# A small row copy moved into free bytes of the last weight slot, and the order of the final matmuls pinned (one Trainium2 core, one-token decode block)

## The chip, the cores and the metric

The kernel runs on one core of one Trainium2 chip. The metric is the device time of one execution in microseconds (us). In the profile PE is the TensorE matmul engine, PEld its weight loads, DVE is VectorE, ACT is ScalarE, SP issues most transfers. "Half clock" means that the clock granted to TensorE was 0.5 of full speed; the trace records each such period.

Each execution has two lengths: the time (outside view) and the span (first to last instruction in the records). All runs quoted were classed fast.

## The reference

One new token `x` (1 x 1024) goes through two branches that are added:

```python
xn = layernorm(x)
# A: grouped-query attention; 32 query heads, 4 key/value heads, 65536 cached keys, Dh = 128
q = xn @ wq;  p = softmax(q @ k.T * Dh**-0.5);  a = (p @ v) @ wo
# B: a mixer, then an MLP with w3 (1024 x 3584) and w4 (3584 x 1024)
h  = gelu(layernorm(xn) @ w1);  x1 = xn + (h, shifted) @ w2
b  = x1 + gelu(layernorm(x1) @ w3) @ w4
out = x + a + b
```

Nearly all of it is reading caches and weights: 169.87 MB for a single row of output.

## The kernel before

Weights and caches come through three slots of 64 KB per partition, one after another in one DMA queue. The last items are the last key block, `wo`, the last value block V7, and `w4` in eight pieces. The slot of `w4` is the one the last key block leaves.

```python
W4_PIECES = (6, 5, 6, 4, 3, 2, 1, 1)      # rows of w4 per transfer, 28 in all
# ...
    def row_acc(j, lhsT, rhs, start=False):
        nc.tensor.matmul(psB[32 * j:32 * j + 32, :], lhsT=lhsT.to_broadcast([lhsT.shape[0], 32]), rhs=rhs, start=start,
                         stop=False, tile_position=(0, 32 * j), skip_group_check=True)
# ... the final value block, inside compute_v
        for e in range(SUBS):
            for t in range(16):
                q = t % 4
                nc.tensor.matmul(oacc[32 * q:32 * (q + 1), :], lhsT=pT[:, e, 32 * t:32 * (t + 1)],
                                 rhs=vt[:, :, e, t, :], start=(e == 0 and t < 4),
                                 stop=(e == SUBS - 1 and t >= 12), tile_position=(0, 32 * q))
        st.done(("V", u))
# ...
        nc.vector.scalar_tensor_tensor(out=og[:], in0=oacc[:], scalar=wb[:, 1:2], in1=og[:],
                                       op0=ALU.mult, op1=ALU.add)
        group_rows(g, og, ol)
```

`row_acc` adds rows into the output accumulator `psB`. `group_rows` masks and sums `og` on DVE (`ol`), gathers the sums over partitions with one matmul (`pm_e`), and normalises to `oT` for the last head group. Before that, `o_acc` collects the output projection of the other three head groups; `add_projection` copies it out of PSUM and adds it to `psB`.

```python
    def add_projection():
        rows = ppool.tile([1, 2, 512], F32, name="o_rows", tag="p")
        nc.vector.tensor_copy(out=rows[:], in_=tail["rows"][0:1, 0:2, :])
        for j in range(2):
            row_acc(j, ident_f[0:1, 0:1], rows[0:1, j, :])

    def compute_w4(lo, hi):
        wt = st.tiles["w4"]
        for c in range(lo, hi):
            for j in range(2):
                row_acc(j, hT[:, c:c + 1], wt[:, D * c + 512 * j:D * c + 512 * (j + 1)])
# ...
    compute_k(NU - 1)
    tail["rows"] = ps_S.tile([P, SUBS, 512], F32, name="o_acc", tag="sc")
    for g in range(HKV - 1):
        project(g)
    add_projection()
    compute_v(NU - 1)
    early = sum(W4_PIECES[:2])
    compute_w4(0, early)
    project(HKV - 1)
    compute_w4(early, FC - NARROW)
```

The tile `o_rows` comes from pool `psb`, tag `p`. It has a single buffer, and this buffer holds `p_sb`, the softmax weights that the value matmuls read. So the copy must wait for the last value matmul. After `psB` a short tail follows: `psB` is copied to `sums`, added to the last six `w4` rows in `pm_r`, cast, stored.

Of the kernel before, what the change touches and what calls it, by code (L numbers as in the profile page):

```python
# [9 lines left out]
F32 = mybir.dt.float32  # L10
# [7 lines left out]
SUBS = 4  # L18
SETS = 4
SLOTS = 3  # L20
W4_PIECES = (6, 5, 6, 4, 3, 2, 1, 1)
NARROW = 6
AHEAD = 3

# [70 lines left out]
def kernel(  # L95
# [14 lines left out]
    nc = tc.nc  # L110
# [3 lines left out]
    D = A_x.shape[-1]  # L114
    S = A_x.shape[1]
    HKV = A_k_cache.shape[1]
    SK = A_k_cache.shape[2]
    DH = A_k_cache.shape[3]
# [3 lines left out]
    FC = F // P  # L122
    UKEYS = P * ROW // DH
    assert DH == P and HQ // HKV == 8 and HKV == 4 and D == 1024 and F == 3584 and S == 1
    assert SK % UKEYS == 0 and sum(W4_PIECES) == FC
    NB = SK // UKEYS
    NU = HKV * NB
# [6 lines left out]
    ppool = ctx.enter_context(tc.tile_pool(name="psb", bufs=1))  # L134
# [14 lines left out]
    class Stream:  # L149
# [17 lines left out]
        def load(self, it):  # L167
# [13 lines left out]
            elif it == "w4":  # L181
                w4_v = B_w4.rearrange("(m c) n -> m c n", c=FC)
                c0 = 0
                for n in W4_PIECES:
                    go(out=t[:, c0 * D:(c0 + n) * D], in_=w4_v[:, c0:c0 + n, :].rearrange("p c n -> p (c n)"))
# [7 lines left out]
    st = Stream()  # L193
# [6 lines left out]
    ident_f = const.tile([P, P], F32, name="ident_f")  # L200
# [9 lines left out]
    for b in range(2):  # L210
        nc.gpsimd.tensor_copy(
            out=spread[:, 2 * b:2 * b + 2, :].rearrange("p r (a i) -> p r a i", a=4),
            in_=ident_f[:, 64 * b:64 * b + 64].rearrange("p (i r) -> p r i", r=2).unsqueeze(2).to_broadcast([P, 2, 4, 32]))
# [6 lines left out]
    psB = ps_B.tile([P, 512], F32, name="psB")  # L220

    def row_acc(j, lhsT, rhs, start=False):
        nc.tensor.matmul(psB[32 * j:32 * j + 32, :], lhsT=lhsT.to_broadcast([lhsT.shape[0], 32]), rhs=rhs, start=start,  # L223
                         stop=False, tile_position=(0, 32 * j), skip_group_check=True)

    x_t = ppool.tile([P, DC, 32], BF16, name="x_t", tag="p")
    for a in range(4):
        nc.vector.transpose(out=x_t[32 * a:32 * a + 32].rearrange("p c j -> p (c j)"),  # L228
                            in_=x_row[:, 256 * a:256 * (a + 1)].rearrange("p (i c) -> p c i", c=DC))
# [3 lines left out]
    def layernorm(src, tag):  # L233
# [37 lines left out]
    sel8big = const.tile([P, P], F32, name="sel8big")  # L271
    nc.vector.tensor_copy(out=sel8big[:].rearrange("p (h d) -> p h d", d=16),
                          in_=sel8[:].unsqueeze(2).to_broadcast([P, 8, 16]))
# [8 lines left out]
    for j in range(2):  # L282
        row_acc(j, ident_f[0:1, 0:1], accx[0:1, 512 * j:512 * (j + 1)], start=True)
# [104 lines left out]
    def group_weights():  # L388
        nball = group["nball"]
        negmg = small.tile([P, 1], F32, name="negmg")  # L390
        nc.vector.tensor_reduce(out=negmg[:], in_=nball[:], axis=AX.X, op=ALU.min)
        wb = small.tile([P, NB], F32, name="wb")
        nc.scalar.activation(out=wb[:], in_=nball[:], func=ACTF.Exp, bias=negmg[:, 0:1], scale=-1.0)
        og = group["og"]
        nc.vector.tensor_scalar(out=og[:], in0=og[:], scalar1=wb[:, 0:1], scalar2=None, op0=ALU.mult)
        lw = small.tile([P, NB], F32, name="lw")
        ol = small.tile([P, DH + 1], F32, name="ol")
        nc.vector.tensor_tensor_reduce(out=lw[:], in0=group["lall"][:], in1=wb[:], scale=1.0, scalar=0.0,
                                       op0=ALU.mult, op1=ALU.add, accum_out=ol[:, DH:DH + 1])
        return og, wb, ol  # L400
# [3 lines left out]
    def compute_v(u):  # L404
        g, b = divmod(u, NB)
        if b == 1:
            og, wb, ol = group_weights()
        vt = st.tiles[("V", u)][:].rearrange("p (s u t d) -> p s u t d", u=SUBS, s=SETS, t=16)
        oacc = ps_O.tile([P, 512], F32, name="oacc")
        pT = group["p"]  # L410
        for e in range(SUBS):
            for t in range(16):
                q = t % 4
                nc.tensor.matmul(oacc[32 * q:32 * (q + 1), :], lhsT=pT[:, e, 32 * t:32 * (t + 1)],  # L414
                                 rhs=vt[:, :, e, t, :], start=(e == 0 and t < 4),
                                 stop=(e == SUBS - 1 and t >= 12), tile_position=(0, 32 * q))
        st.done(("V", u))
        if b == 0:
            og = ogpool.tile([P, 512], F32, name="og", tag="og")
            nc.scalar.copy(out=og[:], in_=oacc[:])  # L420
            group["og"] = og
            return
        nc.vector.scalar_tensor_tensor(out=og[:], in0=oacc[:], scalar=wb[:, 1:2], in1=og[:],  # L423
                                       op0=ALU.mult, op1=ALU.add)
        group_rows(g, og, ol)

    oT = {}
    tail = {}

    def group_rows(g, og, ol):  # L430
        pe = ps_M.tile([P, 512], F32, name="pm_e", tag="pm")
        own = og[:].rearrange("p (s d) -> p s d", d=DH)
        nc.vector.tensor_tensor(out=own, in0=own, in1=mask4[:].unsqueeze(2).to_broadcast([P, 4, DH]), op=ALU.mult)
        nc.vector.tensor_reduce(out=ol[:, 0:DH], in_=og[:].rearrange("p (s d) -> p d s", d=DH), axis=AX.X, op=ALU.add)  # L434
        nc.tensor.matmul(pe[:, 0:DH + 1], lhsT=sel8big[:], rhs=ol[:], start=True, stop=True)  # L435
        msk = small.tile([P, 16, 8], F32, name="msk", tag="msk")
        nc.vector.tensor_tensor(out=msk[:], in0=pe[:, 0:P].rearrange("p (dd j) -> p dd j", j=8),
                                in1=mask16[:].unsqueeze(2).to_broadcast([P, 16, 8]), op=ALU.mult)
        o5 = small.tile([P, 8], F32, name="o5")
        nc.vector.tensor_reduce(out=o5[:], in_=msk[:].rearrange("p dd j -> p j dd"), axis=AX.X, op=ALU.add)  # L440
        rl = small.tile([P, 1], F32, name="rl")
        nc.vector.reciprocal(out=rl[:], in_=pe[:, P:P + 1])
        oT[g] = const.tile([P, 8], BF16, name=f"oT{g}")
        nc.vector.tensor_scalar(out=oT[g][:], in0=o5[:], scalar1=rl[:, 0:1], scalar2=None, op0=ALU.mult)

    def project(g):
        wt = st.tiles["wo"][:].rearrange("p (g j n) -> p g j n", g=HKV, j=8)
        for j in range(8):
            for h2 in range(2):
                if g == HKV - 1:  # L450
                    row_acc(h2, oT[g][:, j:j + 1], wt[:, g, j, 512 * h2:512 * (h2 + 1)])
                    continue
                nc.tensor.matmul(tail["rows"][0:1, h2, :], lhsT=oT[g][:, j:j + 1],  # L453
                                 rhs=wt[:, g, j, 512 * h2:512 * (h2 + 1)], start=(g == 0 and j == 0),
                                 stop=(g == HKV - 2 and j == 7), tile_position=(0, 0))

    def add_projection():
        rows = ppool.tile([1, 2, 512], F32, name="o_rows", tag="p")
        nc.vector.tensor_copy(out=rows[:], in_=tail["rows"][0:1, 0:2, :])  # L459
        for j in range(2):  # L460
            row_acc(j, ident_f[0:1, 0:1], rows[0:1, j, :])

    def compute_w4(lo, hi):
        wt = st.tiles["w4"]
# [3 lines that stand above are left out]
# [4 lines left out]
    for u in range(NU - 1):  # L472
        compute_k(u)
        compute_v(u)
    compute_k(NU - 1)
    tail["rows"] = ps_S.tile([P, SUBS, 512], F32, name="o_acc", tag="sc")
    for g in range(HKV - 1):
        project(g)
    add_projection()
    compute_v(NU - 1)  # L480
    early = sum(W4_PIECES[:2])
    compute_w4(0, early)
    project(HKV - 1)
    compute_w4(early, FC - NARROW)
    sums = ogpool.tile([64, 512], F32, name="sums", tag="og")
    nc.scalar.copy(out=sums[:], in_=psB[0:64, :])
    quarters = [ps_M.tile([P, 512], F32, name="pm_r", tag="pm") for _ in range(2)]
# [1 line left out]
    def quarter_acc(lhsT, rhs, start=False):  # L489
        for h in range(2):  # L490
            for j in range(2):
                q = 2 * h + j
                nc.tensor.matmul(quarters[h][32 * q:32 * q + 32, 0:256], lhsT=lhsT(j), rhs=rhs(j, h), start=start, stop=False,
                                 tile_position=(0, 32 * q), skip_group_check=True)

    def narrow_rows(lo, hi, start=False):
        wt = st.tiles["w4"]
        for c in range(lo, hi):
            quarter_acc(lambda j: hT[:, c:c + 1].to_broadcast([P, 32]),
                        lambda j, h: wt[:, D * c + 512 * j + 256 * h:D * c + 512 * j + 256 * (h + 1)],  # L500
                        start=start and c == lo)

    narrow_rows(FC - NARROW, FC - NARROW + AHEAD, start=True)
    quarter_acc(lambda j: ident_f[0:64, 32 * j:32 * j + 1].to_broadcast([64, 32]),
                lambda j, h: sums[:, 256 * h:256 * (h + 1)])
    narrow_rows(FC - NARROW + AHEAD, FC)

# [4 lines left out]
                        in_=out_t[31:33].rearrange("p h n -> p (h n)"))  # L512
# [29 lines left out]
```

## Time and profile before

| | before |
|---|---|
| time, median of the first three runs | 401.93 us (400.98 to 401.99) |
| span of the profiled execution | 399.0 us |
| mean DMA rate over the span | 426 GB/s |
| PE / DVE / ACT busy | 59% / 52% / 7% |

From the page of the kernel before: the span, the busy share of the DMA engines in 40 slices (tenths, 9 means 90% or more), and the chain of work that ended last, by line.

```profile
span 399.0 us, 2590 instructions
...
DMA  9998999999999999999999999999999999999996
...
DMA big<-in_A_k_cache_dram 42%; DVE big L359 19%; PE sc L364 8%; DMA big<-in_A_wq_dram 5%; PE oacc L414 5%; PE o_acc L453 3%; DVE mx L369 3%; ACT p_sb L382 3%; DVE p_sb L385 2%; PE psB L223 2%; PE psq L289 1%; DVE m L373 0%; PE pm_mx L371 0%; PE pm_mx L378 0%
...
```

DMA is busy at 9 in 38 of 40 slices, so the stream sets the pace of the whole. The chain line does not contradict this: it follows releasers, and inside the stream it goes through waits on slots.

The tail, from the timeline of the kernel before. Columns: start us, length us, engine, line, operation, output<-input, count; the bracket gives the idle time before and who ended it.

```profile
...
384.41 1.21 DVE L459 COPY o_rows<-o_acc 1x1024 f32<-1x1024 f32 x1 [14.25 <-PE oacc L414]
385.55 0.73 DVE L423 SCALAR_TENSOR_TENSOR og<-oacc,wb,og 128x512 f32<-128x512 f32 x1
...
385.68 1.05 PE L223 MATMUL psB<-o_rows,ident_f 1*32 1x512 f32 x4 [1.33 <-DVE o_rows L459]
...
386.65 1.95 PE L223 MATMUL psB<-big,hT 128*32 128x512 bf16 x10
...
388.53 0.80 PE L435 MATMUL pm_e<-ol,sel8big 128*128 128x129 f32 x2
...
395.46 0.58 ACT L486 COPY sums<-psB 64x512 f32<-64x512 f32 x1 [27.91 <-PE psB L223]
...
396.66 0.51 PE L493 MATMUL pm_r<-big,hT 128*32 128x256 bf16 x12
...
397.25 0.43 DVE L510 CAST out_t<-pm_r 64x256 bf16<-64x256 f32 x1 [6.91 <-PE pm_r L493]
...
```

The copy (L459) starts 0.02 us after the last value matmul, which ends at 384.39. PE then idles 1.33 us for it, and `og` (L423), which needs only the value matmuls, stands behind it on DVE and starts 1.14 us late. The chain of waits of the same kernel over the tail (start us, length us, what):

```profile
...
384.41 1.22 DVE o_rows L459
...
385.68 2.92 PE psB L223 x14
388.60 0.73 PE pm_e L435 x2
389.33 5.57 PE psB L223 x45
...
395.46 0.59 ACT sums L486
...
396.09 1.13 PE pm_r L493 x20
...
397.25 0.43 DVE out_t L510
```

No DMA appears in it. The landing records of the trace (when the last of 16 engines reported each transfer):

| transfer | V7 | w4 piece 1 | 2 | 3 | 4 | 5 | 6 | 7 | 8 |
|---|---|---|---|---|---|---|---|---|---|
| rows of w4 | | 6 | 5 | 6 | 4 | 3 | 2 | 1 | 1 |
| landed, us | 379.27 | 382.96 | 386.05 | 389.73 | 392.22 | 394.12 | 395.38 | 396.04 | 396.68 |

The last four matmuls, which need piece 8, start at 396.89 and end at 397.17, 0.50 us after it landed.

### The profile page before, as it was taken

The numbers are of one execution on the slowest core, as the hardware profiler recorded it, in microseconds if no ns is written. First come the engines' busy times: TensorE is split into PE (matmuls) and PEld (weight loads), VectorE is DVE, ScalarE is ACT, GpSimd is POOL, SyncE is SP. The second block draws the span as 40 slices with busy tenths as digits, with TensorE's granted clock in tenths as the row PEclk, the third lists the DMA queues.
The fourth block names the chain that finished last, engine by engine and source line by source line (L and its number), as shares of the span: only waits on it lengthen the run. The fifth ranks groups of instructions, "written<-read, shape, count | busy, mean of one in ns | idle before, by whom it ended". The sixth has DMA issues, their size and how long they took to land.

```text
span 399.0 us, 2590 instructions
## 1 busy us (share of the span) xinstructions
PE 234.1 (59%) x1368; PEld 45.6 (11%) x874; DVE 209.4 (52%) x155; ACT 27.6 (7%) x36; POOL 5.3 (1%) x28
## 2 busy tenths in 40 slices
PE   0561960691569237733974296439443945494987
PEld 0210000000200110011001110101010002010133
DVE  0620010965196559634953795269449932884131
ACT  1001010003000200020002000200100020002000
POOL 2000000000000000000000000000000000000000
PEclk9996896696769787966695679569976886598799
DMA  9998999999999999999999999999999999999996
GB/s 421 420 454 372 437 453 473 434 420 420 422 428 420 440 466 435 420 427 427 435 420 440 447 447 420 422 420 447 427 442 440 440 420 394 425 450 447 393 420 255
DMA packets 4576, 170.03 MB, mean 426 GB/s; under 512 B 467, under 2 KB 469, under 8 KB 982
## 3 DMA queue, kind: packets, MB, share of 16 engines
q1 hardware_dynamic: 4560, 169.87, 98.9%
q8 instruction: 9, 0.15, 0.2%
q14 instruction: 1, 0.01, 0.0%
q10 hardware_dynamic: 6, 0.00, 0.0%
HBM read 169.87 MB, written 0.00 MB: 426 GB/s over the span
## 4 chain that ended last, share of the span: by engine, by line
DMA 48%; DVE 25%; PE 21%; ACT 3%; another core or an unknown queue 2%; issue 1%; DVEq 0%; ACTq 0%
DMA big<-in_A_k_cache_dram 42%; DVE big L359 19%; PE sc L364 8%; DMA big<-in_A_wq_dram 5%; PE oacc L414 5%; PE o_acc L453 3%; DVE mx L369 3%; ACT p_sb L382 3%; DVE p_sb L385 2%; PE psB L223 2%; PE psq L289 1%; DVE m L373 0%; PE pm_mx L371 0%; PE pm_mx L378 0%
## 5 line engine op out<-in xcount | busy, mean ns | idle before, releaser
L364 PE MATMUL sc<-big,qdiag 128*128 128x512 bf16 x512 | 130.2, 416 | 64.2 <-DVE big L359 63.9
L359 DVE STREAM_TRANSPOSE big<-big 128x4096 f32<-128x4096 f32 x32 | 139.4, 4413 | 50.7 <-DMA big<-in_A_k_cache_dram 50.7
L414 PE MATMUL oacc<-big,p_sb 128*32 128x512 bf16 x512 | 45.1, 522 | 34.5 <-DVE p_sb L385 34.5
L369 DVE TENSOR_REDUCE mx<-sc 128x1 f32<-128x2048 f32 x8 | 18.3, 2292 | 30.4 <-PE sc L364 30.4
L364 PEld LDWEIGHTS <-qdiag 128*128 128x128 bf16 x128 | 13.2, 103 | 176.7 <-issue 146.4
L382 ACT ACTIVATE p_sb<-sc,nball 128x2048 bf16<-128x2048 f32 x8 | 15.7, 1967 | 218.3 <-DVE nball L380 218.3
L385 DVE STREAM_TRANSPOSE p_sb<-p_sb 128x2048 bf16<-128x2048 bf16 x8 | 18.5, 2312 | 18.0 <-ACT p_sb L382 18.0
L414 PEld LDWEIGHTS <-p_sb 128*32 128x32 bf16 x512 | 16.8, 126 | 59.5 <-DVE p_sb L385 35.1
L289 PE MATMUL psh<-big,ln_rep_b 128*32 128x512 bf16 (+1 forms) x64 | 12.4, 941 | 8.6 <-DMA big<-in_B_w_dram 8.6
L453 PE MATMUL o_acc<-big,oT 128*1 128x512 bf16 x48 | 13.5, 453 | 2.4 <-ACT p_sb L382 2.4
L371 PE MATMUL pm_mx<-ident_f,mx 128*1 128x128 f32 x8 | 2.2, 270 | 19.1 <-DVE mx L369 19.1
L328 DVE STREAM_TRANSPOSE h_row<-h_row 128x896 bf16<-128x896 bf16 x1 | 1.1, 1111 | 21.7 <-ACT h_row L327 21.7
L423 DVE SCALAR_TENSOR_TENSOR og<-oacc,wb,og 128x512 f32<-128x512 f32 x4 | 3.0, 746 | 15.2 <-PE oacc L414 15.2
L459 DVE COPY o_rows<-o_acc 1x1024 f32<-1x1024 f32 x1 | 1.2, 1212 | 14.2 <-PE oacc L414 14.2
L237 PE MATMUL pm_ln<-ln_rowsum_a,ones_f 128*128 128x1 f32 x2 | 0.6, 347 | 12.6 <-DVE ln_rowsum_a L235 12.6
L435 PE MATMUL pm_e<-ol,sel8big 128*128 128x129 f32 x8 | 2.6, 414 | 7.9 <-DVE ol L434 7.9
L313 POOL COPY qdiag<-qx 32x32 bf16<-32x32 bf16 x16 | 3.2, 203 | 279.2 <-PE sc L364 250.5
L228 DVE STREAM_TRANSPOSE x_t<-x_row 32x256 bf16<-32x256 bf16 x4 | 2.5, 616 | 8.2 <-DMA x_row<-in_A_x_dram 8.1
L223 PE MATMUL psB<-big,hT 128*32 128x512 bf16 x44 | 6.5, 448 | 0.0
L289 PE MATMUL psq<-big,ln_rep_a 128*32 128x512 bf16 x64 | 5.2, 499 | 1.1 <-DMA big<-in_A_wq_dram 1.1
L378 PE MATMUL pm_mx<-ident_f,rep 1*128 1x1 f32 x8 | 1.9, 235 | 5.0 <-DVE rep L375 5.0
L420 ACT COPY og<-oacc 128x512 f32<-128x512 f32 x4 | 2.3, 585 | 34.3 <-PE oacc L414 34.3
(101 smaller groups left out, 75.1 us busy)
## 6 DMA issues: line engine op xcount, KB each, us to landing
big<-in_A_wo_dram SPq DMA_DIRECT2D x1, 8192.0 KB, 36.8
big<-in_B_w_dram SPq DMA_DIRECT2D x1, 7168.0 KB, 38.1
big<-in_B_w_dram SPq DMA_DIRECT2D x2, 2048.0 KB, 45.9
big<-in_B_w_dram SPq DMA_DIRECT2D x2, 1536.0 KB, 27.3
big<-in_B_w_dram SPq DMA_DIRECT2D x1, 1280.0 KB, 24.1
big<-in_B_w_dram SPq DMA_DIRECT2D x1, 1024.0 KB
big<-in_B_w_dram SPq DMA_DIRECT2D x1, 768.0 KB, 30.8
big<-in_B_w_dram SPq DMA_DIRECT2D x1, 512.0 KB, 31.6
```

Of the source, the lines that this page charges most:

```text
L223: nc.tensor.matmul(psB[32 * j:32 * j + 32, :], lhsT=lhsT.to_broadcast([lhsT.shape[0], 32]), rhs=rhs, start=start, stop=False, tile_positio ...
L289: nc.tensor.matmul(acc[32 * q:32 * q + 32, i, 0:n], lhsT=rep[:, c, :], rhs=cols(c, i, q), start=(c == 0), stop=(c == DC - 1), tile_positio ...
L313: nc.gpsimd.tensor_copy(out=qdiag[at, LEAD:].rearrange("p (x c) -> p x c", x=4)[:, :, 32 * a:32 * a + 8], in_=qx[at, :, 8 * g:8 * g + 8])
L359: nc.vector.transpose(out=words, in_=words)
L364: nc.tensor.matmul(sc[:, e, :], lhsT=qdiag[:, c0:c0 + P], rhs=cols[:, s, e, :, b2, :, r], start=(s == 0 and b2 == 0 and r == 0), stop=(s = ...
L369: nc.vector.reduce_max(out=mx[:], in_=sc[:].rearrange("p e n -> p (e n)"), axis=AX.X)
L382: nc.scalar.activation(out=p_sb[:], in_=sc[:], func=ACTF.Exp, bias=nball[:, b:b + 1], scale=SCALE, accum_out=group["lall"][:, b:b + 1])
L385: nc.vector.transpose(out=flat, in_=flat)
L414: nc.tensor.matmul(oacc[32 * q:32 * (q + 1), :], lhsT=pT[:, e, 32 * t:32 * (t + 1)], rhs=vt[:, :, e, t, :], start=(e == 0 and t < 4), stop ...
L423: nc.vector.scalar_tensor_tensor(out=og[:], in0=oacc[:], scalar=wb[:, 1:2], in1=og[:], op0=ALU.mult, op1=ALU.add)
L435: nc.tensor.matmul(pe[:, 0:DH + 1], lhsT=sel8big[:], rhs=ol[:], start=True, stop=True)
L453: nc.tensor.matmul(tail["rows"][0:1, h2, :], lhsT=oT[g][:, j:j + 1], rhs=wt[:, g, j, 512 * h2:512 * (h2 + 1)], start=(g == 0 and j == 0), ...
```

## The change

The copy gets a home that nobody reads: `w4` fills 28 x 1024 of the 32768 columns of its slot, and the copied row goes into the columns behind. (The row is the projected output of three head groups.) It then has to wait only for `o_acc`, and can run while the value matmuls run. Three ordering clauses pin the order on PE: copied rows after the value matmuls, `w4` rows from 5 on after the gathered sums, rows from 11 on after the last head group's projection.

```diff
+FIRST = 5
+AT_ONCE = 2
# ...
+    def copy_projection():
+        tail["o"] = st.tiles["w4"][0:1, FC * D:FC * D + 2 * D].bitcast(F32)
+        nc.vector.tensor_copy(out=tail["o"].rearrange("p (j n) -> p j n", j=2), in_=tail["rows"][0:1, 0:2, :])
+
     def add_projection():
-        rows = ppool.tile([1, 2, 512], F32, name="o_rows", tag="p")
-        nc.vector.tensor_copy(out=rows[:], in_=tail["rows"][0:1, 0:2, :])
         for j in range(2):
-            row_acc(j, ident_f[0:1, 0:1], rows[0:1, j, :])
+            row_acc(j, ident_f[0:1, 0:1], tail["o"][:, 512 * j:512 * (j + 1)])
# ... (compute_v, group_rows and project now return or keep their last matmul)
-    add_projection()
-    compute_v(NU - 1)
-    early = sum(W4_PIECES[:2])
-    compute_w4(0, early)
-    project(HKV - 1)
-    compute_w4(early, FC - NARROW)
+    copy_projection()
+    summed = compute_v(NU - 1)
+    with tc.issue_after(summed):
+        add_projection()
+    early = sum(W4_PIECES[:AT_ONCE])
+    compute_w4(0, FIRST)
+    with tc.issue_after(tail["gathered"]):
+        compute_w4(FIRST, early)
+    projected = project(HKV - 1)
+    with tc.issue_after(projected):
+        compute_w4(early, FC - NARROW)
```

The changed kernel has the same instructions in the same order on PE and DVE as before. The only differences are where the copied row lies and that the copy no longer waits for the value matmuls.

More of the change, by code (lines that the diff above doesn't have):

```diff
@@ L222, in row_acc @@
     def row_acc(j, lhsT, rhs, start=False):
-        nc.tensor.matmul(psB[32 * j:32 * j + 32, :], lhsT=lhsT.to_broadcast([lhsT.shape[0], 32]), rhs=rhs, start=start,
-                         stop=False, tile_position=(0, 32 * j), skip_group_check=True)
+        return nc.tensor.matmul(psB[32 * j:32 * j + 32, :], lhsT=lhsT.to_broadcast([lhsT.shape[0], 32]), rhs=rhs, start=start,
+                                stop=False, tile_position=(0, 32 * j), skip_group_check=True)
     x_t = ppool.tile([P, DC, 32], BF16, name="x_t", tag="p")
@@ L413, in compute_v @@
                 q = t % 4
-                nc.tensor.matmul(oacc[32 * q:32 * (q + 1), :], lhsT=pT[:, e, 32 * t:32 * (t + 1)],
-                                 rhs=vt[:, :, e, t, :], start=(e == 0 and t < 4),
-                                 stop=(e == SUBS - 1 and t >= 12), tile_position=(0, 32 * q))
+                mm = nc.tensor.matmul(oacc[32 * q:32 * (q + 1), :], lhsT=pT[:, e, 32 * t:32 * (t + 1)],
+                                      rhs=vt[:, :, e, t, :], start=(e == 0 and t < 4),
+                                      stop=(e == SUBS - 1 and t >= 12), tile_position=(0, 32 * q))
         st.done(("V", u))
@@ L425, in compute_v @@
         group_rows(g, og, ol)
+        return mm.ins
     oT = {}
@@ L434, in group_rows @@
         nc.vector.tensor_reduce(out=ol[:, 0:DH], in_=og[:].rearrange("p (s d) -> p d s", d=DH), axis=AX.X, op=ALU.add)
-        nc.tensor.matmul(pe[:, 0:DH + 1], lhsT=sel8big[:], rhs=ol[:], start=True, stop=True)
+        tail["gathered"] = nc.tensor.matmul(pe[:, 0:DH + 1], lhsT=sel8big[:], rhs=ol[:], start=True, stop=True).ins
         msk = small.tile([P, 16, 8], F32, name="msk", tag="msk")
@@ L450, in project @@
                 if g == HKV - 1:
-                    row_acc(h2, oT[g][:, j:j + 1], wt[:, g, j, 512 * h2:512 * (h2 + 1)])
+                    mm = row_acc(h2, oT[g][:, j:j + 1], wt[:, g, j, 512 * h2:512 * (h2 + 1)])
                     continue
@@ L455, in project @@
                                  stop=(g == HKV - 2 and j == 7), tile_position=(0, 0))
+        return mm.ins if g == HKV - 1 else None
+    def copy_projection():
+        tail["o"] = st.tiles["w4"][0:1, FC * D:FC * D + 2 * D].bitcast(F32)
+        nc.vector.tensor_copy(out=tail["o"].rearrange("p (j n) -> p j n", j=2), in_=tail["rows"][0:1, 0:2, :])
     def add_projection():
-        rows = ppool.tile([1, 2, 512], F32, name="o_rows", tag="p")
-        nc.vector.tensor_copy(out=rows[:], in_=tail["rows"][0:1, 0:2, :])
         for j in range(2):
-            row_acc(j, ident_f[0:1, 0:1], rows[0:1, j, :])
+            row_acc(j, ident_f[0:1, 0:1], tail["o"][:, 512 * j:512 * (j + 1)])
     def compute_w4(lo, hi):
```

## The prediction

> **What bounds the kernel now.** The page's DMA line stands at 9 (90% or more busy) in 38 of 40 slices, and the mean is 426 GB/s over a 399.0 us span. The Trainium skill, "DMA: Bandwidth & Descriptors", Specifications, gives a fabric ceiling of 435 GB/s; the trace agrees that little is left. So the stream sets the pace, and only the tail after its end is compute. The change touches only the tail.
>
> **The tail, from the timeline and the landing records of before.** The last value block lands at 379.27 us. The eight w4 pieces land at 382.96, 386.05, 389.73, 392.2, 394.12, 395.38, 396.04 and 396.68. PE finishes the value matmuls at 384.39. DVE then does the COPY o_rows, 1.21 us, and PE sits idle 1.33 us until it ends; og starts 1.14 us late. The copy waits for the value matmuls only because its buffer is p_sb's. The chain of waits shows it: oacc, o_rows (1.22 us), then psB and pm_r to the end, no DMA after. Read alone, it promises 1.2 us.
>
> **What the change does.** It removes that wait: o_acc is complete at about 380.9, so the copy (same 1.2 us, same place in DVE's order) runs under the value matmuls, ending near 382.1. The instruction order of PE and DVE is unchanged; no matmul, no DMA and no byte is added. So PE should start on the projection rows near 384.42 instead of 385.68, and og near 384.41 instead of 385.55; the gathered sums (pm_e) near 387.0 instead of 388.53.
>
> **How much is critical.** Little. The last w4 piece lands at 396.68, and the last four matmuls of before, which need it, start at 396.89: PE is only about 0.2 us behind the DMA. With an otherwise empty PE they could start about 0.05 us after landing (as the sixth piece's row does, 395.43 after 395.38). So the gain is about 0.16 us of the 1.2; the rest turns into PE waits for pieces five (394.12), six, seven and eight. The DMA waits on nothing that moves: the w4 pieces are issued once the last key block's slot is free and earlier loads have landed.
>
> It can be more where PE lags further behind the loads. In the profiled run PE was at half clock from 387.07 to 390.49 (projection-row pairs every 427 ns instead of 216 ns; the Trainium skill, "TensorE: Matmul & The Clock Gate", Back-to-back issue gap, gives N/1.2 ns and N/2.4 + 2.5 ns, and the trace agrees). A run in which the throttle holds one more 3.4 us period would be PE-bound at the end, and there up to 1.2 us comes back.
>
> **Prediction: 401.2 us, 80% range 400.3 to 402.0.** Expected true gain 0.2 to 0.5 us. Chances: faster by over 2% 0.01, within 2% 0.98, slower by over 2% 0.01.
>
> **What the profile would show.** Right: COPY at about 381 to 382, inside the value matmuls, released by o_acc; no PE gap after 384.4; sums near 394.7 to 395.0 instead of 395.46; new PE waits on w4 loads at the end, the last four matmuls within 0.1 us of the last landing; chain of waits ending in DMA. Wrong: the COPY still after 384.4; PE still without waits on w4 and the end 1 us earlier against the last landing; w4 landings that moved against the start of their stream.
>
> **What would make it wrong.** Throttle periods falling elsewhere in the tail, as PE now works in other stretches (either sign, about 1 us); DMA rate varying between runs by more than 0.2%; a wait of the copy on the w4 load that I have overlooked.

## The result, and the profile after

| | before | after |
|---|---|---|
| time, median of 6 runs | 401.26 us | 401.33 us (400.88 to 401.81) |
| ratio after / before | | 0.9998, 95% interval 0.9984 to 1.0012 |
| span of the profiled execution | 399.0 us | 399.1 us |
| last value matmul ends | 384.39 | 383.63 |
| row copy starts | 384.41 | 380.17 |
| gathered sums (`pm_e`) start | 388.53 | 386.25 |
| `psB` complete, `sums` starts | 395.46 | 394.85 |
| last w4 piece landed | 396.68 | 396.92 |
| last matmul ends (after that landing) | 397.17 (0.50) | 397.25 (0.33) |

Ratios here and below are the mean time of one kernel's fast runs over that of the other's from the same rounds, so they are not quite the ratio of the medians. In the page after:

```profile
span 399.1 us, 2590 instructions
...
DMA big<-in_A_k_cache_dram 32%; DVE big L361 19%; DMA big<-in_A_v_cache_dram 10%; PE sc L366 8%; PE oacc L416 6%; DMA big<-in_A_wq_dram 6%; DMA big<-in_B_w_dram 4%; DVE p_sb L387 3%; DVE mx L371 3%; ACT p_sb L384 3%; PE psq L291 1%; DVE m L375 0%; PE pm_mx L373 0%; PE pm_mx L380 0%
...
```

The chain now includes the value block's loads (10%) and those of `w4` (4%), which it did not before. The timeline of the tail after:

```profile
...
380.17 1.21 DVE L463 COPY big<-o_acc 1x1024 f32<-1x1024 f32 x1 [9.48 <-PE o_acc L456]
...
383.52 1.05 PE L225 MATMUL psB<-big,ident_f 1*32 1x512 f32 x4
383.65 0.75 DVE L425 SCALAR_TENSOR_TENSOR og<-oacc,wb,og 128x512 f32<-128x512 f32 x1 [2.27 <-PE oacc L416]
...
384.50 1.26 PE L225 MATMUL psB<-big,hT 128*32 128x512 bf16 x10
...
386.25 0.49 PE L438 MATMUL pm_e<-ol,sel8big 128*128 128x129 f32 x2 [0.50 <-DVE ol L437]
...
390.03 1.47 PE L225 MATMUL psB<-big,hT 128*32 128x512 bf16 x12 [0.16 <-DMA big<-in_B_w_dram]
...
392.52 1.04 PE L225 MATMUL psB<-big,hT 128*32 128x512 bf16 x8 [1.02 <-DMA big<-in_B_w_dram]
...
394.43 0.39 PE L225 MATMUL psB<-big,hT 128*32 128x512 bf16 x2 [0.86 <-DMA big<-in_B_w_dram]
...
394.85 0.58 ACT L497 COPY sums<-psB 64x512 f32<-64x512 f32 x1 [26.76 <-PE psB L225]
395.67 0.29 PE L504 MATMUL pm_r<-big,hT 128*32 128x256 bf16 x4 [0.63 <-DMA big<-in_B_w_dram]
...
396.45 0.80 PE L504 MATMUL pm_r<-big,hT 128*32 128x256 bf16 x12
...
```

The copy (L463) runs at 380.17, inside the value matmuls. PE starts the copied rows at 383.52 without a gap, and waits 0.50 us for the gathered sums. From 390.03 on PE waits for DMA again and again. The waits of the same stretch, summed (who waited for whom: us in total, times, longest):

```profile
...
PE psB L225 <- DMA big<-in_B_w_dram: 2.0, 3, 1.0
...
PE pm_r L504 <- DMA big<-in_B_w_dram: 0.6, 1, 0.6
...
PE pm_e L438 <- DVE ol L437: 0.5, 1, 0.5
...
```

PE waits 2.6 us in all for pieces of `w4`. And the chain of waits after is one stream of DMA, with the last four matmuls behind it:

```profile
...
379.53 17.39 DMA big<-in_B_w_dram
396.92 0.04 issue
396.96 0.34 PE pm_r L504 x4
397.30 0.02 issue
397.32 0.43 DVE out_t L521
```

Between landing and the end of the last matmul 0.334 us are left instead of 0.495 us (unrounded records), so 0.16 us less. This belongs to this pair of profiles and is no average gain: the kernel before with one more copy (experiment 4) ended 0.334 us after its last landing in its profile, so executions without the change can end there too. Its last load landed 0.24 us later, but so did V7 (379.51 against 379.27): the stream from V7 to the last piece took 17.41 us in both. The shift is older than the tail.

### The profile page after: what moved, and what is told of

It is laid out like the page before. It is cut to its first block, busy times and chain, and to the rows that moved or that the text cites. A ratio compares the mean times of both kernels' runs of the same rounds, so it can differ in the third digit from the quotient of the medians.

```text
span 399.1 us, 2590 instructions
## 1 busy us (share of the span) xinstructions
PE 233.7 (59%) x1368; PEld 45.9 (11%) x874; DVE 209.5 (53%) x155; ACT 27.6 (7%) x36; POOL 5.3 (1%) x28
## 3 DMA queue, kind: packets, MB, share of 16 engines
q1 hardware_dynamic: 4560, 169.87, 98.9%
HBM read 169.87 MB, written 0.00 MB: 426 GB/s over the span
## 4 chain that ended last, share of the span: by engine, by line
DMA 52%; DVE 26%; PE 16%; ACT 3%; another core or an unknown queue 2%; issue 1%; DVEq 0%; ACTq 0%
DMA big<-in_A_k_cache_dram 32%; DVE big L361 19%; DMA big<-in_A_v_cache_dram 10%; PE sc L366 8%; PE oacc L416 6%; DMA big<-in_A_wq_dram 6%; DMA big<-in_B_w_dram 4%; DVE p_sb L387 3%; DVE mx L371 3%; ACT p_sb L384 3%; PE psq L291 1%; DVE m L375 0%; PE pm_mx L373 0%; PE pm_mx L380 0%
## 5 line engine op out<-in xcount | busy, mean ns | idle before, releaser
L456 PE MATMUL o_acc<-big,oT 128*1 128x512 bf16 x48 | 12.2, 420 | 2.4 <-ACT p_sb L384 2.4
L225 PE MATMUL psB<-big,hT 128*32 128x512 bf16 x44 | 5.6, 380 | 2.0 <-DMA big<-in_B_w_dram 2.0
L463 DVE COPY big<-o_acc 1x1024 f32<-1x1024 f32 x1 | 1.2, 1211 | 9.5 <-PE o_acc L456 9.5
```

The lines of the kernel that those rows point to most:

```text
L225: return nc.tensor.matmul(psB[32 * j:32 * j + 32, :], lhsT=lhsT.to_broadcast([lhsT.shape[0], 32]), rhs=rhs, start=start, stop=False, tile_ ...
L456: nc.tensor.matmul(tail["rows"][0:1, h2, :], lhsT=oT[g][:, j:j + 1], rhs=wt[:, g, j, 512 * h2:512 * (h2 + 1)], start=(g == 0 and j == 0), ...
```

## The experiments

Theory A, the prediction's: in both kernels the `w4` stream ends last or nearly so, and the change turns its 1.2 us into slack. Theory B: the copy's wait was never worth anything. Theory C: the chain of PE and DVE bounds the tail, and the gain was eaten by something the change brought. Each run was timed in five rounds beside the kernel before. Spans of the kernel before in these three sessions (11 runs each): 398.7 to 399.2, means 398.90, 398.89 and 398.86.

### 1. Take the stream away: before with a cut w4

Only the first two pieces of `w4` are loaded, and later rows read rows that are there. The arithmetic is wrong on purpose. The comparison with the reference passed all the same: the part of `w4` in the output lies within its tolerance, so that pass says nothing of `w4`.

```diff
-                for n in W4_PIECES:
+                for n in W4_PIECES[:2]:
# ...
-                row_acc(j, hT[:, c:c + 1], wt[:, D * c + 512 * j:D * c + 512 * (j + 1)])
+                row_acc(j, hT[:, c:c + 1], wt[:, D * (c % 11) + 512 * j:D * (c % 11) + 512 * (j + 1)])
# and the same in narrow_rows
```

> The kernel before, but only the first two w4 pieces (11 of 28 rows) are loaded, and the matmuls of rows 11 to 27 read rows 0 to 16 modulo 11 instead; same matmuls, wrong result on purpose. 4.5 MB less is loaded, about 10.4 us of the stream (pieces three to eight landed from 386.30 to 396.92). Theory A (in both kernels the w4 stream, not the chain of PE and DVE, ends last or nearly so): the end is now PE-bound. In the profiled run of before PE was only 0.2 us behind the loads, after a throttled stretch, so this gains little: 0 to 1.5 us, depending on where half clock falls. No wait of PE on a w4 load past the second piece. Theory B (the copy's wait was never worth anything, since DVE or PE lose the 1.2 us again elsewhere): about the same gain here, and no difference between this and the changed kernel with the same cut. The PE idle of 1.3 us on the copy stays in both theories.

Measured: ratio 0.9959 (0.9937 to 0.9981), which is 1.6 us and a little over the expected 0 to 1.5; spans 396.3 to 398.8, mean 397.60. By span this is 1.30 us less than the kernel before, with a spread of 2.5 us. Its timeline:

```profile
...
383.96 1.21 DVE L459 COPY o_rows<-o_acc 1x1024 f32<-1x1024 f32 x1 [13.78 <-PE oacc L414]
...
385.23 1.05 PE L223 MATMUL psB<-o_rows,ident_f 1*32 1x512 f32 x4 [1.33 <-DVE o_rows L459]
...
386.21 2.32 PE L223 MATMUL psB<-big,hT 128*32 128x512 bf16 x10
...
```

The copy and PE's 1.33 us of idling are there. The first ten `w4` matmuls (L223, at 386.21) take 2.32 us, and 1.26 us in the changed kernel: half clock ran from 386.16 to 389.57. The slowest span of this PE-bound tail, 398.8, just reaches the span of the kernel with its stream. So the kernel before had between 0.1 and 2.6 us of slack, 1.3 us in the mean (398.9 less each span of the cut kernel, an estimate across different executions).

### 2. The changed kernel with the same cut

The edit is the same, on the changed kernel.

> The changed kernel with the same cut of w4 to 11 loaded rows; wrong result on purpose. Theory A: with the stream out of the way the 1.2 us of the change come back, so this is 0.8 to 1.6 us faster than the kernel before with the same cut, and 1.0 to 3 us faster than the kernel before; from the end of the value matmuls to the end of the last matmul about 10.7 us at full clock, against 11.9 us in the other. Theory B: within 0.3 us of the kernel before with the same cut.

Measured: ratio 0.9924 (0.9911 to 0.9937); spans 395.6 to 396.6, mean 396.12. That is 1.48 us less than the cut kernel before. In its timeline:

```profile
...
383.81 1.05 PE L225 MATMUL psB<-big,ident_f 1*32 1x512 f32 x4
...
384.79 1.26 PE L225 MATMUL psB<-big,hT 128*32 128x512 bf16 x10
...
```

From the end of the value matmuls to the end of the last matmul this profile has 10.4 us (383.92 to 394.29), the cut kernel before 12.7 us (383.94 to 396.68) with half clock in it; 10.7 and 11.9 at full clock had been expected. Take the stream away and the change is worth 1.5 us; leave it there and it is worth nothing. Theory B falls. The slack of the changed kernel, worked out in the same way, is 2.3 to 3.3 us.

### 3. Spend the slack: one extra copy after the change

```diff
+        if u == NU - 1:
+            spare = st.tiles["w4"][0:1, FC * D + 2 * D:FC * D + 4 * D].bitcast(F32)
+            for _ in range(1):
+                nc.vector.tensor_copy(out=spare.rearrange("p (j n) -> p j n", j=2),
+                                      in_=oacc[0:1, :].unsqueeze(1).to_broadcast([1, 2, 512]))
         nc.vector.scalar_tensor_tensor(out=og[:], in0=oacc[:], ...
```

> The changed kernel with one more DVE copy of 1x1024 f32 (1.2 us estimated from the copy of the same size) between the value matmuls and og, so that the gathered sums and all PE work behind them come 1.2 us later. The result stays right. Theory A: PE has 1.2 us (if a half-clock period falls into the tail) to 2.8 us (if none does) to spare on the loads, so the time stays within 0.3 us of the changed kernel; PE's waits on w4 shrink by as much. Theory C (the chain of PE and DVE bounds the tail, and the change's gain was eaten by something else it brought): 1.2 us slower than the changed kernel.

Measured: ratio 0.9994 (0.9982 to 1.0006); spans 398.8 to 399.1, mean 398.88. The extra copy took 1.21 us and cost nothing. In its waits, the delay went into PE's wait for `ol` and came out of the waits on `w4`:

```profile
...
PE pm_e L443 <- DVE ol L442: 1.6, 1, 1.6
...
PE psB L225 <- DMA big<-in_B_w_dram: 1.5, 2, 0.9
...
```

Against the changed kernel, the wait on `ol` rose from 0.5 to 1.6 us, and the wait of `psB` on loads fell from 2.0 to 1.5. Theory C falls.

### 4. The mirror: the same extra copy before the change

The row copy goes back to the buffer of `p_sb`. By the build, the three ordering clauses alone change nothing: without the extra copy this kernel is, instruction for instruction on PE, DVE, ACT and SP, the kernel before. It was therefore built and not run.

> The mirror of the first dose: the changed kernel with its copy put back into the buffer of the softmax weights (by the build, then instruction for instruction the kernel before on every engine), and with the same extra DVE copy of 1x1024 f32 ahead of og. Theory A: before the change PE has no slack on the loads where a half-clock period falls into the tail (0.2 us behind in the profile), and about 1.2 us where none does; so the same 1.2 us that cost the changed kernel nothing costs here: 0.3 to 1.2 us slower than the kernel before on average, and in a profile with half clock in the tail PE ends over 1 us after the last load. Rival (there is slack on both sides, and the change altered neither): within 0.2 us of the kernel before.

Measured: ratio 1.0029 (1.0007 to 1.0051); spans 398.8, 399.0, 399.8, 400.3, 400.9, 401.0, mean 399.97. By span the same 1.2 us cost 1.08 us on average here, and nothing after the change. The profile caught the fastest of the six (398.8):

```profile
...
386.19 2.31 PE L225 MATMUL psB<-big,hT 128*32 128x512 bf16 x10
...
388.79 0.80 PE L443 MATMUL pm_e<-ol,sel8big 128*128 128x129 f32 x2 [0.28 <-DVE ol L442]
...
389.52 1.48 PE L225 MATMUL psB<-big,hT 128*32 128x512 bf16 x12
...
```

PE did run at half clock here, from 386.16 to 389.57, but a part of this fell on its wait for the sums. Its last matmul ended 0.33 us after the last landing. So the expectation of a profile more than 1 us late was not met; the slower runs have no profile.

### 5. Four and two extra copies after the change

The edit of experiment 3 with `range(4)` and `range(2)`.

> The same with four such copies, 4.8 us later. Theory A: past the slack, so the time rises by 4.8 us less the slack of 1.2 to 2.8 us: 2.0 to 3.6 us slower than the changed kernel, PE no longer waits for w4. Theory C: 4.8 us slower. If DMA alone set the end, with no bound to the slack: 0.

Measured: ratio 1.0104 (1.0088 to 1.0119); spans 402.7 to 404.1, mean 403.30. By span that is 4.4 us more than the kernel before for 4.9 us of copies: above the expected 2.0 to 3.6, and close to what theory C had said. If the slack were a fixed 2.8 us (398.9 less 396.1), it should have cost 2.1 us.

> The changed kernel with two extra copies (2.4 us) ahead of og. Four copies cost 4.3 us of 4.8 by the means, one cost nothing. Theory A with a knee that depends on the clock: with full clock to the end about 0 to 0.3 us, with a half-clock period in the tail 1.2 to 1.7 us slower; on average 0.2 to 1.6 us slower than the changed kernel, with a wide spread. If the cost is a straight line through the four-copy point: 2.1 us slower.

Measured: ratio 1.0038 (1.0022 to 1.0053); spans 399.6 to 400.7, mean 400.15, so 1.26 us more for 2.46 us of copies. From two copies to four the mean span rose by 3.15 us for some 2.4 us of copies, more than the copies themselves. The profile shows half clock coming in with the delay:

```profile
...
388.73 0.49 PE L443 MATMUL pm_e<-ol,sel8big 128*128 128x129 f32 x2 [2.85 <-DVE ol L442]
...
389.15 2.60 PE L225 MATMUL psB<-big,hT 128*32 128x512 bf16 x12
...
391.53 2.50 PE L225 MATMUL psB<-big,oT 128*32 128x512 bf16 x16
...
```

PE waited 2.85 us for the sums. At 389.34, 0.6 us after it resumed, half clock began and lasted to 392.75. Twelve matmuls took 2.60 us here and 1.47 us in the changed kernel. With four copies PE waited 5.34 us, and half clock held for 6.83 us (390.46 to 397.29). So the slack is real, but it shrank where a half-clock period followed a long wait of PE; experiment 7 takes up whether the wait brings it. My expectation for four copies had left that out.

### 6. The copy without the ordering clauses

```diff
-    with tc.issue_after(summed):
-        add_projection()
+    add_projection()
# and the other two clauses likewise
```

> The changed kernel without its three ordering clauses; by the build, the two matmuls that add the copied rows then stand ahead of the value matmuls on PE and wait for the copy, and the gathered sums stand two row pairs later. PE then idles about 1.2 us before the value matmuls, and og comes about 2.2 us later after the end of o_acc. Theory A: within the slack at full clock, past it with a half-clock period: 0 to 1.2 us slower than the changed kernel. If the ordering clauses carried the change's whole worth and the tail were bound by PE: 2.2 us slower.

Measured: ratio 1.0023 (1.0008 to 1.0039); spans 398.7 to 400.6, mean 399.95: 1.06 us more than the kernel before, within what was expected. In the timeline of its fastest run, the one profiled:

```profile
...
379.83 1.21 DVE L463 COPY big<-o_acc 1x1024 f32<-1x1024 f32 x1 [9.48 <-PE o_acc L456]
...
381.10 1.05 PE L225 MATMUL psB<-big,ident_f 1*32 1x512 f32 x4 [1.30 <-DVE big L463]
...
382.07 3.64 PE L416 MATMUL oacc<-big,p_sb 128*32 128x512 bf16 x64
...
```

The scheduler put the two `psB` matmuls ahead of the value matmuls. PE waited 1.30 us for the copy there, and the value matmuls started at 382.07 instead of 379.56. (The trace shows each of the two as two.) This execution itself still ended with the loads; what the slower ones spent was not profiled. The clauses alone change nothing and the copy alone loses a microsecond; together they break even.

### 7. Why the cut kernel before is 1.5 us slower, not 1.2

Six useless matmuls keep PE busy while the copy runs (cut kernel before, `w4` cut as in 1):

```diff
+        if u == NU - 1:
+            spare = ps_M.tile([P, 512], F32, name="pm_fill", tag="pm")
+            with tc.issue_after(mm.ins):
+                for n in range(6):
+                    mm = nc.tensor.matmul(spare[:], lhsT=qdiag[:, LEAD:LEAD + P],
+                                          rhs=st.tiles["wo"][:, 512 * n:512 * (n + 1)], start=True, stop=True)
         st.done(("V", u))
```

> Why is the cut kernel before not just 1.2 us but 1.5 us slower than the cut changed kernel, and spread over 2.5 us of span (396.3 to 398.8) where the other spreads over 1.0 (395.6 to 396.6)? Its profile has a half-clock period of 3.4 us starting 2.3 us after PE fell idle behind the copy; the profile of the cut changed kernel has none. This is the cut kernel before with six matmuls of 128x512 (about 1.3 us at full clock, of no use, into an unused PSUM bank) right after the value matmuls, so that PE is busy while the copy runs; nothing else moves on any engine. Theory H (the idle PE brings the half clock): no half-clock period in the tail, spans of 396.2 to 397.2 with a spread like the cut changed kernel's, so 0.3 to 1 us faster on average than the cut kernel before though it does more work, with the 1.2 us of the copy itself still in. Rival (the half clock falls as it will, or the filling work itself brings it): the same mean and spread as the cut kernel before, or slower.

Measured: ratio 0.9952 (0.994 to 0.9964); spans 396.3 to 397.5, mean 396.93. There is no half clock in its tail before 397.67:

```profile
...
382.79 1.47 PE L423 MATMUL pm_fill<-big,qdiag 128*128 128x512 bf16 x6
...
384.19 1.05 PE L225 MATMUL psB<-o_rows,ident_f 1*32 1x512 f32 x4
...
```

> The cut kernel before once more, beside the filled one on the same chip: mean span near 397.6, spread 2 us or more. Its second profile should show the copy behind the value matmuls, PE idle 1.33 us, and either a half-clock period in the tail (span 398 or more) or none (span near 396.4).

Measured on the same chip: ratio 0.9979 (0.996 to 0.9999); spans 396.9, 396.9, 397.0, 398.6, 398.7, 398.7, mean 397.80. Its profile has span 398.7, the 1.33 us gap, and half clock from 386.36 to 389.77.

Doing more work made the tail 0.87 us faster by mean span. The cut kernel before had spans of 398.4 or more in 6 of its 12 runs, the filled one in 0 of 6. This supports that the idle PE behind the copy brings the half-clock period. How long an idle stretch it takes is not settled. The profiles read as follows (half clock after 380 us; PE gaps between the end of `o_acc` and the last projection):

| kernel | PE gaps, us | half clock |
|---|---|---|
| before | 1.33 | 387.07 to 390.49 |
| cut before, first and second profile | 1.33; 1.33 | 386.16 to 389.57; 386.36 to 389.77 |
| before + one copy (4) | 1.33, 0.28 | 386.16 to 389.57 |
| after + two copies | 2.85 | 389.34 to 392.75 |
| after + four copies | 5.34 | 390.46 to 397.29 |
| after | 0.50 | none before 398.65 |
| cut after | 0.50 | none before 396.43 |
| after + one copy | 1.59 | none before 397.40 |
| without clauses | 1.30, 1.35 | none before 398.32 |
| cut and filled | 0.32 | none before 397.67 |

Length alone does not sort them: 1.33 us was followed by half clock in four profiles of four, 1.59 us and 1.30 + 1.35 us were not. How the gap lies against the clock's periods, and what the matmuls around it were, may both play a part; one profile each cannot tell.

A rival is excluded only in part. In the six profiles with half clock in the tail, the half-clock period before it had ended at 372.27 to 373.42; in four of the five without, at 370.10 to 371.34 (the filled kernel: 370.37). So the end of that earlier period sorts the profiles nearly as well as the gap does. The fifth speaks for the gap: in the cut changed kernel the earlier period ended at 372.54, much as in the first profile of the cut kernel before (372.50), and with a gap of 0.50 us instead of 1.33 no half clock followed. That the gap brings it is supported, not shown.

## Why the prediction was right

- **No change in time.** Predicted 401.2 us (400.3 to 402.0) and within 2%; measured 401.33 us, ratio 0.9998. That the two lie 0.13 us apart is partly luck: the median of the kernel before had been 401.93 us over the three runs known then and was 401.26 over six, and the expected gain did not show.
- **The bound.** "PE is only about 0.2 us behind the DMA" held. The distance from the last landing to the end of the last matmul fell by 0.16 us in this pair of profiles, as predicted. The timing cannot show this: its interval is 0.28% wide, over 1 us. Only the profiles do.
- **Where the 1.2 us went.** They turned into PE's waits for `w4`. These sum to 2.6 us, more than 1.2, for two further reasons: the profile of before had 3.4 us of half clock in its tail and the one after had none, and in the one after the value matmuls ended 0.76 us earlier while the last load landed 0.24 us later. So PE waited not only for the pieces from the fifth on, as predicted, but already for the third (0.16 us) and the fourth (1.02 us). Experiments 1 and 2 give them back by removing the stream; 3 and 4 show the same 1.2 us free on one side and costing 1.08 us on the other.
- **Steps of the tail.** Copy under the value matmuls, no gap before the copied rows, `sums` between 394.7 and 395.0, and last matmuls within 0.1 us of the last landing all hold: 380.17, none, 394.85 and 0.04 us. The copy came before the 381 to 382 that were named, and `pm_e` came at 386.25, not 387.0, because `o_acc` and the value matmuls themselves ended 0.8 us earlier in this execution: the half clock under which part of `o_acc` ran ended at 371.34 instead of 373.42. From the end of the value matmuls the distance to `pm_e` was 2.62 us, against some 2.6 predicted.
- **What did not hold.** "Expected true gain 0.2 to 0.5 us" rested on executions in which one more half-clock period makes the tail PE-bound, "and there up to 1.2 us comes back". None was seen: 33 spans of the kernel before lie between 398.7 and 399.2. Even the cut kernel before, with half clock in its tail, ended at 398.8 at most. The mean span of the six runs after was 399.05, so no gain is shown outside the one pair of profiles. (A slip of words: the pairs 427 ns apart that the prediction calls projection rows are rows of `w4` in the trace.)
- **What the prediction did not know.** It held that the throttle might fall elsewhere. It did not say that the copy's own gap could be what brings it, which experiment 7 supports.

## What to carry to other kernels

A chain of waits names the last releaser at each step, not how close the next one was: before pricing a wait on it, compare the last consumer with the landing of the load it needs. If a wait removed moves nothing, cut the suspected other bound in both kernels and spend the supposed slack on purpose; the pair of answers settles where the gain went. No version faster than both came out of this: with PE already waiting for the loads, what is left of this tail is the stream and the third of a microsecond after its last landing. In the profile of before the 16 DMA engines reported piece 8 between 394.74 and 396.68, so besides fewer bytes or a faster stream, an even finish of the engines might shorten it; that was not tried.

## What the Trainium skill lacked or had wrong

- "TensorE: Matmul & The Clock Gate", Why this matters for your kernels, advises no PE gaps of over about 3 us. Here half clock followed a PE gap of 1.33 us in four profiles of four and did not follow one of 1.59 us, so a limit on the gap's length does not describe these runs; that the gap was the cause is supported, not shown. The page's free-running window of 3413 ns does fit (What's actually happening): the half-clock periods in the tail lasted 3.41 or 6.83 us and began 13.65 or 17.07 us after the one before had ended, 4 or 5 such windows.
- "DMA: Bandwidth & Descriptors", Where 436 GB/s comes from, says that for transfers from HBM to SBUF the HBM side, about 358 GB/s, binds. This kernel read 169.87 MB from HBM at a mean of 426 GB/s over its whole span, near the page's fabric ceiling of 435 GB/s; one core was in use. Only that sentence misleads: just after it the page calls its own 425 GB/s near the fabric rate, and the note to its measured table (Measured) keeps the 358 GB/s for both cores of a pair streaming.
- The pages time single transfers by size; no page has the cost of a small piece queued right behind other loads. In the kernel before, a `w4` row took 0.615 us in the first six-row piece (landed 382.96, after 379.27) and 0.64 us in the last one-row piece (396.68, after 396.04), 4% more, with 2048 bytes per partition.
